# Second batch's operands replaced behind the token tiles; fourth chunk of the first mixture in another order

## The chip, the cores and the metric

The kernel runs on one core of a Trainium2 chip. The metric is device time in microseconds for one execution of the whole program. Engines are named as in the profile: PE is TensorE, PEld its weight loads, DVE is VectorE, ACT is ScalarE, POOL is GpSimd, SP is SyncE, which issues the DMAs.

## The reference, cut to what matters

An attention with a cluster mask, then two mixtures; every product is computed to float32 accuracy.

```python
def reference(...):
    x = _attn_ref(q, k, v, centroids)        # 2 batches x 8 heads, 768 tokens, head 64
    x = x.transpose(0, 2, 1, 3).reshape(1536, 512)
    h = x @ w_in                             # first mixture: 512 -> 2048
    r = np.maximum(h, 0.0)
    x = (r * r) @ w_out                      # 2048 -> 512
    p = domain_probs / (domain_probs.sum(-1, keepdims=True) + 1e-09)
    for e in range(4):                       # second mixture: 4 experts
        h = np.maximum(x @ w1[e], 0.0)       # 512 -> 1024
        out += p[:, e:e + 1] * (h @ w2[e])   # 1024 -> 512
```

## The kernel before

**Numbers as pairs.** An operand of TensorE is kept as a pair: hi is the value cast to TensorE's format (a cast on ScalarE), lo is what the cast left over (a subtraction on VectorE or GpSimd). A product is three matmuls: hi by hi, hi by lo, lo by hi. The h or l at the end of a tile's name says which half it is (wxh, wxl).

**Products of blocks.** The first matrix product of either mixture is done on a 2x2 split with seven block products instead of eight. For that, sums and differences of the blocks are needed on both sides. On the weights' side they are made by `w_sums` (four operations on GpSimd) and `w_mixed` (cast and subtraction into wyh and wyl); on the tokens' side by `t_sum`, with `r_hi` (cast, L943) and `r_lo` (subtraction, L946). The list `PROD` names the products: 1 takes RB11, 5 takes RT1, 6 RT2, 2 RB21, 7 RT3, 4 RT4, and 3 RB22.

**First mixture.** The 2048 hidden units are done in eight chunks (c = 0 to 7) of 256. `chunk(c)` is a generator of 15 pieces x = 0 to 14, each TensorE work (`prod1`, `gemm2`, `plain`) and what follows it. `gemm2` multiplies by w_out into banks 4 to 7, and VectorE adds those to x (L912). Between the pieces, hooks run that `put(c, x)` has hung there: the conversion of the next chunk's weights. `conv_in(c + 1)` prepares w_in (two blocks p and q, the sums, the two mixed operands mix), `conv_out(c + 1)` w_out (op and oq). The weights lie in memory as 64-bit words, so the conversion of a block (`split64`) is five integer operations on VectorE into a scratch tile (cva or fa), a cast on ScalarE, and a subtraction. `relu_c(c, tb, f)` takes one bank or sum: relu, square and cast on ScalarE (L845 to L847), the lo half on GpSimd (L848). `relu_c(c, 1, 1)` reads bank A of the chunk directly, and that bank is written again by `plain`, L856.

**Second mixture.** It goes through 32 groups n. Groups 0 to 15 are the 16 slices of 256 hidden units for the first 768 tokens (batch 0), 16 to 31 the same for batch 1 (NFQ is 16). A group's TensorE work stands in this order: product 4 of group n-1 (in `fourth`), product 1 of n, product 3 of n-1 (in `third`), then products 5, 6, 2 and 7 of n, each six matmuls of 128x384 (L878); then the six token tiles of group n-1, each six matmuls of 128x512 (L1040), whose result VectorE adds to x (L1050). Between them stand the preparation of the weights of group n+1: `raws` (wxh, wxl, L981), the sums (L200 to L203), `mixed` (wyh on ScalarE, wyl on GpSimd, L208 and L209); and wzl of group n, `second_lo` on GpSimd, L994. `c_copy` (L1009) is the copy out of bank A by ScalarE, `c_add` (L1012) an addition on VectorE.

**The second batch's operands.** Batch 1 needs the seven token operands anew. Four of them (RT3, RT1, RT2, RB21) go to a tile of their own, rt, during groups 11 to 14. The other three replace batch 0's in place, in xa: RB11, RT4 and RB22. Each may be overwritten only when the product that reads it has run for group 15. `swapped(n, i, eng)` does that in group 15 and at the start of group 16: RB11 behind product 1 of group 15, with the subtraction on VectorE; RT4 behind product 4 of group 15, the subtraction on GpSimd; RB22 behind product 3 of group 15, on VectorE. Products 4 and 3 of group 15 run within the head of group 16. RB11 is next read in group 16, by product 1; RT4 and RB22 are next read in the head of group 17, by products 4 and 3 of group 16.

**Order.** Nothing is reordered by a scheduler: each engine takes its instructions in the order in which the code is written, and waits on semaphores where data or a buffer is not there yet. What stands early in an engine's queue and waits holds up what stands behind it.

## Time and profile before

| | us |
|---|---|
| median of 3 runs | 1016.59 (1016.07 to 1016.91) |
| profiled execution, its own time | 1016.18 |
| its span in the profile | 1014.20 |
| TensorE busy | 1000.7 |
| VectorE busy | 733.2 |
| GpSimd busy | 620.0 |
| ScalarE busy | 561.3 |

The span is the stretch that the trace covers; the rest of the execution's time lies around it. Busy times are averages over very different parts: attention until about 260 us, the first mixture from then until about 509 us (L856 first at 264.4, the last L906 at 508.6), the second mixture behind that. Matmuls overlap, so a row's duration is not the distance to the next: within a group of this kernel, matmuls of 128x384 start some 0.17 us apart and those of 128x512 some 0.23 us. Where a row of a timeline ends in square brackets, the engine was idle ahead of it for that many microseconds, and the name behind the arrow is what it waited for.

### The profile page before, as it was taken

How to read it: one execution, taken by the hardware profiler on the slowest of the kernel's cores; microseconds unless marked ns; L12 is line 12 of the kernel's file. 1: busy time of each engine (PE TensorE's matmuls, PEld its weight loads, DVE VectorE, ACT ScalarE, POOL GpSimd, SP SyncE). 2: the span in 40 equal slices, each digit the busy share in tenths (PEclk: the TensorE clock that was granted, in tenths of full speed). 3: DMA queues.
4: the chain of work that ended last, by engine and by line, in shares of the span. 5: the costliest groups of instructions: out<-in, count | busy, mean ns of one | idle time of the engine just before them, and what ended most of it. 6: DMA issues, size and time to landing. Idle time of an engine off the chain costs nothing.

```text
span 1014.2 us, 15000 instructions
## 1 busy us (share of the span) xinstructions
PE 1000.7 (99%) x5467; PEld 892.1 (88%) x5467; DVE 733.2 (72%) x1114; ACT 561.3 (55%) x1131; POOL 620.0 (61%) x630
## 2 busy tenths in 40 slices
PE   8999999999999999999999999999999999999998
PEld 8999999999888878888889989899888998998997
DVE  7889899888899977988585554667665555555555
ACT  6888888988655644456454344344443444434431
POOL 5567677773326644346576766767667666676671
PEclk9999999999999999999999999999999999999999
DMA  7577876862112122212012122122223221211201
GB/s 184 126 155 178 191 179 157 187 140 71 42 42 83 46 80 83 77 49 82 22 42 84 43 83 83 42 84 63 63 83 104 84 79 47 83 63 62 84 22 63
DMA packets 74066, 89.65 MB, mean 88 GB/s; under 512 B 27316, under 2 KB 50248, under 8 KB 73992
## 3 DMA queue, kind: packets, MB, share of 16 engines
q1 hardware_dynamic: 73992, 88.69, 31.8%
q8 instruction: 43, 0.70, 0.3%
q14 instruction: 31, 0.25, 0.1%
HBM read 62.58 MB, written 3.19 MB: 65 GB/s over the span
## 4 chain that ended last, share of the span: by engine, by line
PE 71%; DVE 18%; POOL 4%; issue 2%; ACT 2%; DMA 1%; SPq 0%; POOLq 0%; DVEq 0%; ACTq 0%
PE bank L1040 26%; PE bank L878 24%; PE bank L906 5%; PE t L678 4%; PE s L645 4%; DVE ptl L684 2%; PE po L692 2%; PE po L694 2%; DVE nb L654 2%; DVE x L912 2%; PE bank L856 1%; DVE fa L177 1%; PE m L469 1%; DVE fa L172 1%; DVE cva L167 1%
## 5 line engine op out<-in xcount | busy, mean ns | idle before, releaser
L1050 DVE SCALAR_TENSOR_TENSOR x<-bank,pe_p,x 128x512 f32<-128x512 f32 x180 | 135.2, 751 | 69.6 <-PE bank L1040 69.3
L981 POOL TENSOR_TENSOR wxl<-raw,wxh 128x512 fp32r<-128x512 f32 x64 | 82.5, 1309 | 142.1 <-ACT wxh L980 142.1
L208 ACT CAST wyh<-raw 128x512 fp32r<-128x512 f32 x64 | 39.6, 621 | 152.9 <-POOL raw L201 120.0
L1040 PE MATMUL bank<-wzh,gb 128*128 128x512 f32 x384 | 121.2, 390 | 0.0
L1040 PE MATMUL bank<-wzh,ga 128*128 128x512 f32 x384 | 121.1, 390 | 0.0
L1012 DVE TENSOR_TENSOR fa<-bank,fa 128x384 f32<-128x384 f32 x96 | 53.3, 556 | 86.5 <-PE bank L878 57.3
L684 DVE TENSOR_TENSOR ptl<-t,pth 128x384 fp32r<-128x384 f32 x192 | 98.1, 549 | 17.9 <-ACT pth L683 17.4
L878 PE MATMUL bank<-xa,wxh 128*128 128x384 f32 (+1 forms) x392 | 103.9, 346 | 0.0
L654 DVE TENSOR_REDUCE nb<-s 128x1 f32<-128x768 f32 x96 | 90.9, 947 | 10.9 <-PE s L645 10.2
L878 PE MATMUL bank<-xa,wyh 128*128 128x384 f32 (+1 forms) x344 | 89.0, 339 | 1.6 <-ACT fa L1009 1.5
L665 ACT ACTIVATE p<-s,nb 128x768 f32<-128x768 f32 x96 | 87.9, 916 | 2.1 <-DVE nb L654 1.9
L683 ACT CAST pth<-t 128x384 fp32r<-128x384 f32 x192 | 83.9, 486 | 9.2 <-PE t L678 8.4
L678 PE MATMUL t<-identf,p 128*128 128x128 f32 x576 | 85.7, 276 | 1.2 <-DVE ptl L684 1.0
L645 PE MATMUL s<-k,q 80*128 80x384 f32 (+1 forms) x384 | 85.9, 345 | 0.5 <-DMA k<-ohm 0.5
L1040 PEld LDWEIGHTS bank<-wzh,gb 128*128 128x128 f32 x384 | 72.1, 188 | 14.7
L1040 PEld LDWEIGHTS bank<-wzh,ga 128*128 128x128 f32 x384 | 72.1, 188 | 14.7
L209 POOL TENSOR_TENSOR wyl<-raw,wyh 128x512 fp32r<-128x512 f32 x64 | 84.7, 1344 | 0.0
L1009 ACT COPY fa<-bank 128x384 f32<-128x384 f32 x96 | 46.0, 480 | 64.5 <-PE bank L878 64.4
L692 PE MATMUL po<-pth,vv 128*128 128x256 f32 x288 | 80.4, 309 | 0.0
L906 PE MATMUL bank<-gb,wzh 128*128 128x512 f32 x240 | 78.0, 391 | 0.3 <-DVE x L912 0.2
L678 PEld LDWEIGHTS t<-identf,p 128*128 128x128 f32 x576 | 67.1, 140 | 11.9 <-DVE ptl L684 9.0
L878 PEld LDWEIGHTS bank<-xa,wxh 128*128 128x128 f32 x392 | 72.2, 188 | 5.6
(279 smaller groups left out, 2648.8 us busy)
## 6 DMA issues: line engine op xcount, KB each, us to landing
raw<-in_moe_w_dram SPq DMA_DIRECT2D x64, 512.0 KB, 3.6
raw<-in_moe_w_in_dram SPq DMA_DIRECT2D x7, 1024.0 KB, 5.2
raw<-in_moe_w_out_dram SPq DMA_DIRECT2D x6, 1024.0 KB
k<-nkh SPq DMA_DIRECT2D x28, 192.0 KB, 3.4
q<-nqh SPq DMA_DIRECT2D x28, 192.0 KB, 4.1
nv<-in_v_dram SPq DMA_DIRECT2D x16, 192.0 KB, 3.8
out_dram<-x SPq DMA_DIRECT2D x12, 256.0 KB, 2.0
k<-nkl SPq DMA_DIRECT2D x14, 192.0 KB, 3.1
```

The source lines that it names most:

```text
L209: eng.tensor_tensor(lo, a[m], hi.bitcast(F32), op=ALU.subtract)
L645: nc.tensor.matmul(s[:, j, 0:HALF], stk[i, nq][:, t * 128:(t + 1) * 128], stk[i, nk][:, j * HALF:(j + 1) * HALF], start=first, stop=not first)
L654: nc.vector.tensor_reduce(out=nb, in_=s_ps[u][:, :, 0:HALF], axis=AX.XY, op=ALU.max, negate=True)
L665: nc.scalar.activation(p, s_ps.pop(u)[:, :, 0:HALF], AF.Exp, bias=nb_t.pop(u), accum_out=sums_t[hp][:, i % 2, t:t + 1])
L678: nc.tensor.transpose(tp[:, j], p_sb[u][:, half, j * 128:(j + 1) * 128], identf)
L683: return (lambda: nc.scalar.copy(dh, tp), lambda: nc.vector.tensor_tensor(dl, tp, dh.bitcast(F32), op=ALU.subtract))
L684: lambda: nc.vector.tensor_tensor(dl, tp, dh.bitcast(F32), op=ALU.subtract))
L692: nc.tensor.matmul(po_t[pr], vt[i][:, kt], pth[:, kt], start=(kt == 0), stop=False)
L878: nc.tensor.matmul(ps, w[:, ks], x(xx)[:, kt], start=(first and kt == 0 and z == 0), stop=(kt == 1 and z == 2), skip_group_check=True)
L906: nc.tensor.matmul(o, a[:, d], b, start=(ft == 0 and z == 0), stop=(ft == 1 and z == 2))
L1040: nc.tensor.matmul(o, a, w[:, f], start=(f == 0 and z == 0), stop=(f == 1 and z == 2))
L1050: nc.vector.scalar_tensor_tensor(out=acc, in0=o, scalar=pc, in1=acc, op0=ALU.mult, op1=ALU.add)
```

## The change

It has two parts. In the first mixture only chunk 3 is touched, with the preparation of chunk 4's weights in it. There the lo half of block q and the four sums go from GpSimd to VectorE; the relu of `relu_c(3, 1, 1)` is split: the relu itself stays behind product 4, and its square, cast and subtraction stand behind the mixed operands, at x = 9, where the cast and subtraction of the mixed operands now also stand; the first conversion of w_out moves from x = 9 to x = 10, and one cast of wzh from x = 12 to the start of chunk 4. In the second mixture the three calls of `swapped` stand behind the token tiles: RB11 at the end of group 15, RT4 and RB22 at the end of group 16, RT4 first. The engine of each stays what it was.

```diff
--- before.py
+++ after.py
@@ -192,11 +192,10 @@
 
     a_t = {}
 
-    def w_sums(a):
+    def w_sums(a, P=nc.gpsimd):
 
         a11, a12 = a[0][:, 0:2], a[0][:, 2:4]
         a21, a22 = a[1][:, 0:2], a[1][:, 2:4]
-        P = nc.gpsimd
         P.tensor_tensor(a22, a21, a22, op=ALU.add)
         P.tensor_tensor(a21, a11, a21, op=ALU.subtract)
         P.tensor_tensor(a11, a22, a11, op=ALU.subtract)
@@ -838,14 +837,20 @@
         x2_t = []
         relus = []
 
-        def relu2(src, c, tb, f):
+        def relu2_parts(src, c, tb, f):
             hh, hl = h_slot(c, tb, f)
             r = mp["r"][:, len(relus) % 2]
             relus.append(0)
             nc.scalar.activation(r, src, AF.Relu)
-            nc.scalar.activation(r, r, AF.Square)
-            nc.scalar.copy(hh, r)
-            nc.gpsimd.tensor_tensor(hl, r, hh.bitcast(F32), op=ALU.subtract)
+
+            def rest():
+                nc.scalar.activation(r, r, AF.Square)
+                nc.scalar.copy(hh, r)
+                nc.gpsimd.tensor_tensor(hl, r, hh.bitcast(F32), op=ALU.subtract)
+            return rest
+
+        def relu2(src, c, tb, f):
+            relu2_parts(src, c, tb, f)()
 
         def plain(c, m, ps, tb=0):
 
@@ -892,9 +897,12 @@
         def add1(c, k, b):
             nc.vector.tensor_tensor(mp["c1"][:, k], bank1(c, b), mp["c1"][:, k], op=ALU.add)
 
+        def relu_parts(c, tb, f):
+            src = bank1(c, "A") if (f, tb) == (1, 1) else mp["c1"][:, {(0, 1): 0, (0, 2): 1, (1, 2): 2}[f, tb]]
+            return relu2_parts(src, c, tb, f)
+
         def relu_c(c, tb, f):
-            src = bank1(c, "A") if (f, tb) == (1, 1) else mp["c1"][:, {(0, 1): 0, (0, 2): 1, (1, 2): 2}[f, tb]]
-            relu2(src, c, tb, f)
+            relu_parts(c, tb, f)()
 
         def gemm2(c, tb, ft, ns=range(4)):
             wh, wl = w_block(1, 2 * (c % 2) + ft)
@@ -1384,17 +1392,19 @@
 
             b = 2 * (c % 2)
             p, q = [split64(c // 2, 0, b + m, lambda shp, m=m: cv_p[m](shp),
-                            (nc.vector, nc.gpsimd)[m]) for m in range(2)]
+                            (nc.vector, nc.gpsimd)[m and c != 4]) for m in range(2)]
 
             def a():
                 return [a_t[c // 2, 0, b + m]["a"] for m in range(2)]
-            return p, q, [lambda: w_sums(a())], [
+            return p, q, [lambda: w_sums(a(), *([nc.vector] if c == 4 else []))], [
                 [lambda m=m: w_mixed(c % 2, m, a(), nc.gpsimd)] for m in range(2)]
 
         def conv_out(c, cvs=cv_p):
             return [
                 split64(c // 2, 1, 2 * (c % 2) + m, lambda shp, m=m: cvs[m](shp), nc.vector)
                 for m in range(2)]
+
+        split = []
 
         def chunk(c):
             yield lambda: prod1(c, 1), lambda: copy1(c, 0)
@@ -1406,7 +1416,8 @@
             yield lambda: c > 2 and gemm2(c - 1, 2, 0), None
             yield lambda: prod1(c, 7), lambda: (copy1(c, 2), add1(c, 2, "C"))
             yield lambda: gemm2(c - 1, 2, 1), lambda: c > 2 and relu_c(c, 2, 1)
-            yield lambda: prod1(c, 4), lambda: relu_c(c, 1, 1)
+            yield lambda: prod1(c, 4), lambda: (
+                split.append(relu_parts(c, 1, 1)) if c == 3 else relu_c(c, 1, 1))
             yield lambda: prod1(c, 3), lambda: (
                 add1(c, 1, "C"), relu_c(c, *((1, 0) if c == 2 else (2, 0))))
             yield lambda: plain(c + 1, 0, bank[3]), lambda: c > 2 and relu2(bank[3], c + 1, 0, 0)
@@ -1467,12 +1478,18 @@
                 put_load(c, 10, 4, 0)
                 put(3, [0], [[lambda: relu2(bank[3], 3, 0, 0)]])
             else:
-                put(c, (4, 5, 5, 5, 7, 7, 7, 7, 7, 7) if c == 3 else (1, 4, 4, 4, 5, 6, 6, 7, 7, 7), [
-                    p[0], p[2][0:1], q[0][0:3], p[2][1:2], q[0][3:5], q[1], sums2,
-                    [lambda c=c: relu_c(c, 1, 0)], *mix])
+                if c == 3:
+                    put(c, (4, 5, 5, 5, 7, 7, 7, 8, 8, 9, 9, 9), [
+                        p[0], p[2][0:1], q[0][0:3], p[2][1:2], q[0][3:5], q[2][0:1],
+                        [lambda: relu_c(3, 1, 0)], q[2][1:2], sums2, *mix, [lambda: split.pop()()]])
+                else:
+                    put(c, (1, 4, 4, 4, 5, 6, 6, 7, 7, 7), [
+                        p[0], p[2][0:1], q[0][0:3], p[2][1:2], q[0][3:5], q[1], sums2,
+                        [lambda c=c: relu_c(c, 1, 0)], *mix])
                 put_load(c, 7, c + 2, 0)
                 op, oq = conv_out(c + 1)
-                put(c, (9, 10, 11, 12), [op[0][0:3], op[0][3:5], oq[0][0:3], op[2][0:1]])
+                put(c, (10 if c == 3 else 9, 10, 11), [op[0][0:3], op[0][3:5], oq[0][0:3]])
+                put(*((c + 1, [0]) if c == 3 else (c, [12])), [op[2][0:1]])
             put(c + 1, (0, 0), [[lambda c=c: relu2(bank[c % 2], c + 1, 0, 1)],
                                 op[2][1:2] if c > 2 else []])
             put(*((c, [13]) if c > 3 else (c + 1, [0])), [oq[0][3:5]])
@@ -1549,16 +1566,14 @@
                     fq_load(3, 0)
                     fq_load(2, 1)
 
-        def swapped(n, i, eng):
-            if n == NFQ - 1:
-                r_hi(1, R_OF[i])
-                r_lo(1, R_OF[i], eng)
+        def swapped(i, eng):
+            r_hi(1, R_OF[i])
+            r_lo(1, R_OF[i], eng)
 
         def fourth(n):
             product(n, 4)
             h_hi(n, 1, 0)
             h_lo(n, 1, 0)
-            swapped(n, 4, nc.gpsimd)
             m = n - (NFQ - 6)
             if 0 <= m < 4:
                 r_hi(1, (RT3, RT1, RT2, RB21)[m])
@@ -1570,7 +1585,6 @@
         def last_relu(n):
             h_hi(n, 0, 1)
             h_lo(n, 0, 1)
-            swapped(n, 3, nc.vector)
 
         def group(n):
             prep = fq_prep(n + 1)
@@ -1579,7 +1593,6 @@
                 fourth(n - 1)
             product(n, 1)
             c_copy(n, 0)
-            swapped(n, 1, nc.vector)
             if n > 1:
                 third(n - 1)
             last_relu(n - 1)
@@ -1606,6 +1619,11 @@
             second_lo(n, nc.gpsimd)
             for t in range(2, NTT):
                 token_tile(n - 1, t)
+            if n == NFQ - 1:
+                swapped(1, nc.vector)
+            if n == NFQ:
+                swapped(4, nc.gpsimd)
+                swapped(3, nc.vector)
             fq_load(n + 3, 0)
             fq_load(n + 2, 1)
             if 0 <= m < 5 and m != 3:
```

In what follows the queues are shown, one engine at a time. The names are those of the code; [waits ...] are the semaphores, by the engine or DMA queue that raises them. Line numbers of the changed kernel are one lower at the sums and the mixed operands, five higher at the block products (L883) and eight higher behind those.

GpSimd, from the last subtraction of group 15's preparation to the head of group 16, before (xa is RT4's lo half):

```order
L209 TENSOR_TENSOR wyl<-raw,wyh 128x512 [waits PE_49,Activation_49]
L994 TENSOR_TENSOR wzl<-raw,wzh 128x1024 [waits DMAHW1_49]
L946 TENSOR_TENSOR xa<-x_4465,xa 128x768 [waits DVE_49,PE_49,Activation_49]
L981 TENSOR_TENSOR wxl<-raw,wxh 128x512 [waits DMAHW2_49,Activation_49]
L981 TENSOR_TENSOR wxl<-raw,wxh 128x256 [waits PE_49,Activation_49]
L200 TENSOR_TENSOR raw<-raw 128x2x128 [waits Pool_49]
```

The same one group later in the changed kernel, from the end of group 16 to the head of group 17:

```order
L208 TENSOR_TENSOR wyl<-raw,wyh 128x512 [waits Activation_49]
L208 TENSOR_TENSOR wyl<-raw,wyh 128x512 [waits PE_49,Activation_49]
L1002 TENSOR_TENSOR wzl<-raw,wzh 128x1024 [waits DMAHW3_49]
L954 TENSOR_TENSOR xa<-x_4465,xa 128x768 [waits DVE_49,Activation_49]
L989 TENSOR_TENSOR wxl<-raw,wxh 128x512 [waits DMAHW4_49,PE_49,Activation_49]
L989 TENSOR_TENSOR wxl<-raw,wxh 128x256 [waits PE_49,Activation_49]
```

RT4's lo half stood behind the wzl of group 15 and now stands behind that of group 16; it no longer waits for TensorE.

VectorE, from the end of group 14's work on the token tiles, before (xa is RB11's lo half, in the head of group 15):

```order
L1050 SCALAR_TENSOR_TENSOR x_4464<-bank_4462,pe_p,x_4464 128x2x256 [waits PE_49]
L1050 SCALAR_TENSOR_TENSOR x_4465<-bank_4463,pe_p,x_4465 128x2x256 [waits PE_49]
L940 TENSOR_TENSOR x_4465<-x_4465,x_4464 128x2x384
L1021 SCALAR_TENSOR_TENSOR gb<-bank_4456,gb 128x384 [waits Activation_49]
L946 TENSOR_TENSOR xa<-x_4464,xa 128x768 [waits PE_49,Activation_49]
L1012 TENSOR_TENSOR fa<-bank_4458,fa 128x384 [waits PE_49]
L1021 SCALAR_TENSOR_TENSOR gb<-fa,gb 128x384 [waits Activation_49]
```

VectorE in the changed kernel, at the end of group 15 and the start of group 16:

```order
L1058 SCALAR_TENSOR_TENSOR x_4464<-bank_4462,pe_p,x_4464 128x2x256 [waits PE_49]
L1058 SCALAR_TENSOR_TENSOR x_4465<-bank_4463,pe_p,x_4465 128x2x256 [waits PE_49]
L954 TENSOR_TENSOR xa<-x_4464,xa 128x768 [waits Activation_49]
L1029 SCALAR_TENSOR_TENSOR ga<-bank_4457,ga 128x384 [waits Activation_49]
L1020 TENSOR_TENSOR fa<-bank_4459,fa 128x384 [waits PE_49]
L1029 SCALAR_TENSOR_TENSOR ga<-fa,ga 128x384 [waits Activation_49]
```

The subtraction stood between the head's two operations in group 15 and now stands behind the last token tile's addition, ahead of the head of group 16.

VectorE in chunk 3, from the last addition of a run of four on, before (cva and fa are the scratch tiles; L161 begins the conversion of w_out):

```order
L912 TENSOR_TENSOR x_4465<-bank_4463,x_4465 128x512 [waits PE_49]
L161 TENSOR_SCALAR cva<-raw 128x512 [waits DMAHW2_49,Pool_49]
L164 TENSOR_SCALAR cva<-cva 128x512 [waits DVE_49]
L167 TENSOR_SCALAR cva<-cva 128x512 [waits DVE_49]
L893 TENSOR_TENSOR fa<-bank_4458,fa 128x512 [waits PE_49]
L172 SCALAR_TENSOR_TENSOR cva<-raw,cva 128x512 [waits DVE_49]
L177 SCALAR_TENSOR_TENSOR cva<-raw,cva 128x512 [waits DVE_49]
```

The same place in the changed kernel:

```order
L920 TENSOR_TENSOR x_4465<-bank_4463,x_4465 128x512 [waits PE_49]
L186 TENSOR_TENSOR wxl<-fa,wxh 128x512 [waits Activation_49]
L199 TENSOR_TENSOR fa<-fa 128x256 [waits DVE_49]
L200 TENSOR_TENSOR fa<-cva,fa 128x256 [waits DVE_49]
L201 TENSOR_TENSOR cva<-fa,cva 128x256 [waits DVE_49]
L202 TENSOR_TENSOR cva<-cva 128x256 [waits DVE_49]
L898 TENSOR_TENSOR fa<-bank_4458,fa 128x512 [waits PE_49]
L161 TENSOR_SCALAR cva<-raw 128x512 [waits DMAHW2_49,Pool_49]
L164 TENSOR_SCALAR cva<-cva 128x512 [waits DVE_49]
L167 TENSOR_SCALAR cva<-cva 128x512 [waits DVE_49]
```

Five operations came in ahead of the conversion, and the addition of bank C (L893, now L898) moved ahead of it too.

## Rows read from the trace of the kernel before

**Rows 1.** Page, part 1: busy us, share of the span, number of instructions.
```profile
PE 1000.7 (99%) x5467; PEld 892.1 (88%) x5467; DVE 733.2 (72%) x1114; ACT 561.3 (55%) x1131; POOL 620.0 (61%) x630
```

**Rows 2.** Waits of TensorE, whole span: us in total, times, longest.
```profile
PE bank L856 <- ACT fa L845: 1.8, 1, 1.8
PE bank L878 <- ACT fa L1009: 1.5, 1, 1.5
...
PE bank L878 <- ACT fa L890: 0.4, 1, 0.4
```

**Rows 3.** Timeline, chunk 3: start, us, line, operation, tiles [idle before <-releaser].
```profile
364.08 2.48 DVE L912 TENSOR_TENSOR x<-bank,x 128x512 f32<-128x512 f32 x4
...
366.05 0.62 ACT L847 CAST gb<-fa 128x512 fp32r<-128x512 f32 x1
...
370.69 1.28 POOL L209 TENSOR_TENSOR wyl<-cva,wyh 128x512 fp32r<-128x512 f32 x1
...
372.00 1.47 DVE L161 TENSOR_SCALAR cva<-raw 128x512 int32<-128x512 int32 x1 [5.44 <-POOL wyl L209]
```

**Rows 4.** Timeline, chunks 3 and 4: adds and idle time of VectorE, matmuls behind.
```profile
389.18 2.48 DVE L912 TENSOR_TENSOR x<-bank,x 128x512 f32<-128x512 f32 x4
...
390.15 0.39 PE L906 MATMUL bank<-gb,wzh 128*128 128x512 f32 x1
...
396.61 0.69 DVE L893 TENSOR_TENSOR fa<-bank,fa 128x512 f32<-128x512 f32 x1 [1.17 <-ACT fa L890]
...
415.06 0.50 PE L906 MATMUL bank<-gb,wzh 128*128 128x512 f32 x1 [0.23 <-DVE x L912]
```

**Rows 5.** Timeline of VectorE: one subtraction of two SBUF tiles, at two places.
```profile
345.49 1.78 DVE L186 TENSOR_TENSOR wzl<-raw,wzh 128x512 fp32r<-128x512 f32 x1
...
361.55 0.69 DVE L186 TENSOR_TENSOR wxl<-cva,wxh 128x512 fp32r<-128x512 f32 x1
```

**Rows 6.** Timeline of TensorE: first matmuls of groups 15, 16 and 17.
```profile
734.39 0.51 PE L878 MATMUL bank<-xa,wxh 128*128 128x384 f32 x2
...
751.63 0.51 PE L878 MATMUL bank<-xa,wxh 128*128 128x384 f32 x2
...
767.13 0.51 PE L878 MATMUL bank<-xa,wxh 128*128 128x384 f32 x2
```

**Rows 7.** Timeline, group 15: VectorE's subtraction and GpSimd's beside it.
```profile
737.62 2.40 POOL L994 TENSOR_TENSOR wzl<-raw,wzh 128x1024 fp32r<-128x1024 f32 x1
...
738.00 2.83 DVE L946 TENSOR_TENSOR xa<-x,xa 128x768 fp32r<-128x768 f32 x1 [1.02 <-ACT xa L943]
```

**Rows 8.** Timeline around the start of group 17: ScalarE's cast, GpSimd's subtractions.
```profile
767.14 2.54 POOL L209 TENSOR_TENSOR wyl<-raw,wyh 128x512 fp32r<-128x512 f32 x2
...
767.21 0.62 ACT L208 CAST wyh<-raw 128x512 fp32r<-128x512 f32 x1 [1.01 <-POOL raw L203]
...
769.64 2.40 POOL L994 TENSOR_TENSOR wzl<-raw,wzh 128x1024 fp32r<-128x1024 f32 x1
```

**Rows 9.** Lines 946 and 943: duration in ns, min/median/max, first and last start.
```profile
L946 DVE TENSOR_TENSOR xa<-x,xa x6: 944/1228/2834, 504.5 to 756.9; 128x768 fp32r<-128x768 f32 x6
L946 POOL TENSOR_TENSOR xa<-x,xa x3: 1837/1846/2201, 496.9 to 756.5; 128x768 fp32r<-128x768 f32 x3
...
L943 ACT CAST xa<-x x9: 817/833/841, 492.2 to 756.0; 128x768 fp32r<-128x768 f32 x9
```

**Rows 10.** Start and end: matmuls; window row: us, busy, granted clock, DMA, GB/s.
```profile
2.65 2.72 PE L1071 MATMUL po<-identr 128*128 128x256 f32 x11 [2.65 <-DVE sel L295]
5.16 1.47 PE L347 MATMUL s<-identf,nk 128*128 128x128 f32 x6
6.44 0.85 PE L347 MATMUL t<-identf,nq 128*128 128x128 f32 x6
...
1009.81 0.39 PE L1040 MATMUL bank<-wzh,ga 128*128 128x512 f32 x1
...
1013.00:1014.20 1.20, 0.00 (x0) 0.67 0.00 0
```

## The prediction

> **What bounds the kernel now.** I read the page's busy shares first: TensorE is busy for 99% of the span, so any time it gains or loses goes to the end almost one to one [rows 1]. Then I read the list of who TensorE waited for. Of its few waits, three stand where the change works: 1.8 us on a relu of the fourth chunk (chunk 3), 0.4 us on a copy at the start of chunk 4, and 1.5 us on a copy in group 15 of the second mixture, the last group of the first batch [rows 2]. If all three went and nothing came in their place, the gain would be 3.7 us and about 0.3 us of restarting the pipeline. The timelines of the other engines say what comes in their place, and that is where I spent the time.
>
> **Part 1: the chunk.** The relu that reads bank 1 now runs ahead of two conversions, so the bank is free before TensorE asks for it, and the copy now runs ahead of the conversion of wzh. Both waits of 1.8 and 0.4 us should go. But VectorE is the next limit. From 372.00 on, when the lo half of wyl has freed the tile cva [rows 3], VectorE works without a gap until 395.4 (its next idle time ends at 396.61 and is 1.17 us long, rows 4), and in that stretch it adds the product's banks to x. Of the run of four adds at 389.18 the first ends near 389.86, and TensorE writes that bank again at 390.15: 0.3 us to spare. One chunk later, at 415.06, TensorE already waits for such an add [rows 4]. So TensorE, freed of 2.2 us in chunk 3, runs into these adds, and what part 1 is worth is how much earlier VectorE's stretch starts or how much shorter it gets, not the 2.2 us.
>
> When does it start? Five operations are new on VectorE ahead of it: the lo half of wxl (0.69 us alone) and four sums of half its width, which no row shows; I bound each by 0.35 us (half) and 0.69 us. They follow the four adds that start at 364.08 and end at 366.6. GpSimd begins its first difference when the cast of 366.05 ends, 366.7 [rows 3], and a second 1.9 us later, as ScalarE needs three passes of 0.63 us for each. VectorE's subtraction of two SBUF tiles takes 0.69 us alone, and 1.78 us where it began during a GpSimd operation [rows 5]: it waited until that one was over. So of the four sums two wait behind GpSimd's two differences (1.3 us each), and the sums end at about 366.6 + 0.6 + 1.2 + 0.3 + 1.4 + 0.3 + 0.9 = 371.1 (lo half, wait, sum, wait, sum, two sums). Then come a cast (0.6) and the lo half of wyl (1.3): the stretch starts at 373.1, 1.1 us later than before. In return the add of bank C (0.6 us, a quarter of a run of adds) is done ahead of it, and GpSimd's last difference meets the adds from PSUM and one short subtraction instead of a longer collision (about 0.8 us less). Sum: 1.1 - 0.6 - 0.8 = **-0.3 us**. Bounds: with no collision in the sums -1.3 us, with one more collision in the stretch +1.0 us. I take -0.3, since rows 5 show the collision for the same kind of operation.
>
> The Trainium skill (SBUF — State Buffer, Who interferes with whom) says that VectorE with two SBUF inputs and GpSimd take turns on one port, whole instructions at a time. By that rule the value is the -0.3 us used here; without it -1.3 us, and the end 1.0 us earlier.
>
> **Part 2: the operands of the second batch.** Three casts on ScalarE and three subtractions (two on VectorE, one on GpSimd) move from just behind the product that last reads the old operand to the end of the group. Nothing is added; each has the same price as before. What counts is how soon TensorE needs them.
>
> *Removed.* In group 15 VectorE's subtraction of xa took 2.83 us because GpSimd's wyl and wzl held it up until 740.02 [rows 7]; alone it takes 0.94 us [rows 9]. Behind it the copy that TensorE waited for was late. Group 15 lasts from 734.39 to 751.63, 17.24 us, and group 16 to 767.13, 15.50 us [rows 6]. Without the subtraction in its head, group 15 should last 15.5 us: **-1.7 us**.
>
> *RB11, first operand of group 16.* Its cast now stands behind the last cast of wyh, and TensorE's second product of group 16 reads it, 1.04 us (six matmuls, some 0.17 us apart in rows 6) after the group starts. Against a group boundary, wyh's last cast starts at +0.08 (767.21 against 767.13) and takes 0.62 us; the cast of xa (0.83 us) ends at +1.4. VectorE's subtraction starts there, but GpSimd's two wyl operations fill +0.0 to +2.5 [rows 8], so it waits for the second and ends 0.81 us behind it (740.83 against 740.02, rows 7): +3.3. The second matmul of that product needs it and would have run at +1.2. **+2.2 us**; without the collision +1.2.
>
> *RT4, first operand of group 17.* Its subtraction stays on GpSimd, and there it now stands behind wyl, wyl and wzl of the end of group 16. These run after the boundary: the two wyl take +0.0 to +2.5, wzl 2.40 us from +2.5 [rows 8]. RB22's subtraction on VectorE, ready at +2.2 after two casts, gets its turn at +2.5 and delays wzl to about +3.2, so wzl ends at +5.6. Then xa's own 1.84 us [rows 9]: ready at +7.4. The very first product of group 17 reads it with its second matmul, wanted at +0.2. **+7.3 us** (6.6 if RB22 doesn't hold up wzl). Queued behind on GpSimd is only wxl, which is not due before late in the group: GpSimd is idle for some 4 us there. RB22 itself is ready at +3.4 and costs nothing next to this. Nothing later can give the time back, since TensorE waits hardly anywhere else.
>
> *The clock.* That is over 7 us in which TensorE does one matmul. At the program's end the granted clock is 1.00 until after 1013 and 0.67 on average over the last 1.2 us, which puts its fall to half (from 2.4 to 1.2 GHz) at 1013.4, 3.2 us after the last matmul. At the start TensorE works from 2.65 on; six matmuls of a kind take 1.47 us at 5.16, and six of the same size 0.85 us at 6.44 [rows 10]. So it worked 3.8 us (2.65 to 6.44) before it ran at full speed, and lost about half of these. I expect the clock to fall in the stall and to come back as it did at the start: 3.8 us at about half speed, **+1.8 us**; bounds 0 (it holds) and 2.6.
>
> **Sum.** -0.3 - 1.7 + 2.2 + 7.3 + 1.8 = +9.3 us. The profiled execution took 1016.18 us (span 1014.20), which gives 1025.5; the median of the three runs is 0.4 above it, and a median is what I predict: 1016.59 + 9.3 = **1025.9 us**.
>
> **Rivals.** *The clock holds through the stall.* Everything else as above: 1024.1 us. For it: the stall is broken by one matmul near +1.5, and only one fall is in the trace; against it: it is twice as long as the idle time before that fall. The Trainium skill (TensorE: Matmul & The Clock Gate, Part 1) has the clock at 1.2 GHz after idling until there has been sustained work, and the trace agrees at both ends; by that rule it is 1025.9. *GpSimd is less far behind.* If only xa and wzl stand after the boundary, the wyl pair being done before it, the big stall is some 4.8 us, too short to be sure of the clock: about 1022. Against it: the pair starts at the boundary in rows 8, as the sums ahead of it are tied to the same group's products. *The other side: faster.* The stall in group 15 goes (-1.7), part 1 gives 1.3 to 2.5, and the moved subtractions are in time: 1012.4 to 1013.6 us. This needs GpSimd to reach xa before TensorE reaches group 17; it decides at the boundary, where wzl would have to be over, and rows 8 show it ending 4.9 us later (772.04 against 767.13). That the order in the queues is not what the change says is shut out by its rows.
>
> **How the numbers follow.** Forecast 0.71, clock holds 0.15, GpSimd less late 0.08, faster 0.03, no change within 0.2% (about what a measurement of this kernel can tell from none) 0.03. The range takes in the clock's rival with part 1 at its best (1024.1 - 1.0 = 1023.1) and the forecast with part 1 at its worst and the clock's upper bound, not both in full (1025.9 + 1.8 = 1027.7): 1022.9 to 1027.8. Faster by over 0.2% 0.03, within 0.2% 0.03, slower 0.94.
>
> **What would show it.** In the profile after, TensorE's list of waits should be led by L883, the product, on GpSimd's xa of L954 (lines of the changed kernel), 5 to 7 us in one piece, at the start of group 17, and a wait of some 2 us on VectorE's xa in the second product of group 16; the waits on the relu and on the copy of group 15 should be gone. In chunks 3 and 4 new waits on the adds (L920), 1 to 2 us in all, should eat what the relu's wait gives back. Matmuls behind the long wait should start nearly twice as far apart as the 0.17 us of rows 6 for a few us, and the granted clock of that stretch should be below 1. If the xa on GpSimd ends before TensorE gets to group 17, the forecast is wrong as a whole.

## The result

The changed kernel took 1025.77 us in the median of 4 runs (1024.73 to 1026.23), the kernel before 1016.41 (1016.07 to 1016.91, 4 runs beside them). The ratio is 1.009, with a 95% interval of 1.0073 to 1.0108: 9.4 us slower. The forecast was 1025.9.

### The profile page after: what moved, and what is told of

Read it like the earlier page. It is cut to its first block, busy times and chain, and to the rows that moved or that the text cites. A ratio compares the mean times of both kernels' runs of the same rounds, so it can differ in the third digit from the quotient of the medians.

```text
span 1024.0 us, 15000 instructions
## 1 busy us (share of the span) xinstructions
PE 1004.5 (98%) x5467; PEld 894.7 (87%) x5467; DVE 734.2 (72%) x1119; ACT 561.2 (55%) x1131; POOL 617.3 (60%) x625
## 4 chain that ended last, share of the span: by engine, by line
PE 71%; DVE 19%; POOL 4%; issue 3%; ACT 2%; SPq 0%; DMA 0%; POOLq 0%; DVEq 0%; ACTq 0%
PE bank L1048 25%; PE bank L883 24%; PE bank L914 5%; PE t L677 4%; PE s L644 4%; DVE ptl L683 2%; PE po L691 2%; PE po L693 2%; DVE nb L653 2%; DVE x L920 2%; PE bank L861 1%; PE m L468 1%; DVE cva L167 1%; DVE fa L177 1%; POOL wyl L208 1%
## 5 line engine op out<-in xcount | busy, mean ns | idle before, releaser
L883 PE MATMUL bank<-xa,wxh 128*128 128x384 f32 (+1 forms) x392 | 105.9, 350 | 8.4 <-POOL xa L954 5.4
L883 PE MATMUL bank<-xa,wyh 128*128 128x384 f32 (+1 forms) x344 | 89.2, 339 | 0.1
L883 PEld LDWEIGHTS bank<-xa,wxh 128*128 128x128 f32 x392 | 73.1, 190 | 15.2 <-POOL xa L954 5.7
## 6 DMA issues: line engine op xcount, KB each, us to landing
raw<-in_moe_w_in_dram SPq DMA_DIRECT2D x7, 1024.0 KB, 5.1
raw<-in_moe_w_out_dram SPq DMA_DIRECT2D x6, 1024.0 KB
```

The lines of the kernel that those rows point to most:

```text
L883: nc.tensor.matmul(ps, w[:, ks], x(xx)[:, kt], start=(first and kt == 0 and z == 0), stop=(kt == 1 and z == 2), skip_group_check=True)
```

## The profile after

TensorE is busy for 1004.5 us (before: 1000.7, [rows 1]) in a span of 1024.0. Its list of waits (us in total, times, longest) of the changed kernel, to be held against [rows 2]:

```profile
PE bank L883 <- POOL xa L954: 5.4, 1, 5.4
...
PE bank L914 <- DVE x L920: 1.9, 3, 1.0
PE bank L883 <- ACT xa L951: 1.6, 2, 1.3
PE bank L883 <- DVE xa L954: 1.5, 1, 1.5
```

The three waits of [rows 2] are gone. In their place stand the moved operands (GpSimd's xa, its cast on ScalarE, VectorE's xa) and VectorE's additions. In what follows, what a stall costs is the distance between the starts of the two matmuls around it less the usual one (0.17 us for 128x384, 0.23 for 128x512); it is some 0.2 us more than the wait in the list.

The timeline of the changed kernel from the end of group 16 into group 17 shows the largest of them (start, us, engine, line, operation, tiles, idle time before):

```profile
767.40 0.39 PE L1048 MATMUL bank<-wzh,ga 128*128 128x512 f32 x1
769.10 0.45 PE L883 MATMUL bank<-xa,wxh 128*128 128x384 f32 x1 [1.31 <-ACT xa L951]
774.95 0.69 PE L883 MATMUL bank<-xa,wxh 128*128 128x384 f32 x1 [5.41 <-POOL xa L954]
...
776.71 0.84 PE L883 MATMUL bank<-xa,wxh 128*128 128x384 f32 x2
...
780.60 0.51 PE L883 MATMUL bank<-rt,wyh 128*128 128x384 f32 x2
...
767.62 2.50 POOL L208 TENSOR_TENSOR wyl<-raw,wyh 128x512 fp32r<-128x512 f32 x2
770.07 3.06 POOL L1002 TENSOR_TENSOR wzl<-raw,wzh 128x1024 fp32r<-128x1024 f32 x1
773.10 1.79 POOL L954 TENSOR_TENSOR xa<-x,xa 128x768 fp32r<-128x768 f32 x1
...
769.81 1.13 DVE L954 TENSOR_TENSOR xa<-x,xa 128x768 fp32r<-128x768 f32 x1 [1.24 <-ACT xa L951]
```

Group 17 could have started at 767.63. One matmul runs at 769.10, when ScalarE's cast is there; the second runs at 774.95, right after GpSimd's xa, which stood behind two wyl and wzl and ended at 774.89, 7.26 us behind the group's start. wzl took 3.06 us instead of the 2.40 of [rows 8], since VectorE's subtraction of RB22 got its turn between wyl and wzl. Behind the stall two matmuls take 0.84 us, later 0.51.

The granted clock of TensorE tells why (window: us, TensorE busy, matmuls, granted clock, DMA share, GB/s):

```profile
771.00:773.00 2.00, 0.00 (x0) 0.91 0.77 261
773.00:774.80 1.80, 0.00 (x0) 0.50 0.35 28
...
776.00:778.00 2.00, 2.00 (x8) 0.50 0.19 67
...
779.00:780.00 1.00, 1.00 (x6) 0.77 0.00 0
780.00:785.00 5.00, 5.00 (x30) 1.00 0.00 0
```

0.91 over two microseconds at the levels 1.0 and 0.5 (2.4 and 1.2 GHz) means that the clock fell at 772.6, 3.5 us after the start of the one matmul in the stall; 0.77 over the last means that it rose at about 779.5, 4.5 us after the work began again. Twelve matmuls in that stretch start 0.32 us apart instead of 0.17, and the first 0.48: 2.1 us in all.

The head of group 16, with RB11:

```profile
749.85 0.51 PE L883 MATMUL bank<-xa,wxh 128*128 128x384 f32 x2
...
753.25 0.44 PE L883 MATMUL bank<-xa,wxh 128*128 128x384 f32 x1 [1.48 <-DVE xa L954]
...
749.86 2.52 POOL L208 TENSOR_TENSOR wyl<-raw,wyh 128x512 fp32r<-128x512 f32 x2
...
751.31 1.88 DVE L954 TENSOR_TENSOR xa<-x,xa 128x768 fp32r<-128x768 f32 x1 [0.51 <-ACT xa L951]
```

VectorE's subtraction is ready to start at 751.31 but ends at 753.19, 0.81 us behind GpSimd's second wyl (752.38); alone it takes 0.94 [rows 9]. The Trainium skill (SBUF — State Buffer, Who interferes with whom) says that a VectorE instruction with two SBUF inputs and a GpSimd instruction that reads SBUF exclude each other; these 1.88 us agree with it, as the sums in chunk 3 do:

```profile
367.68 1.40 DVE L199 TENSOR_TENSOR fa<-fa 128x256 f32<-128x256 f32 x1
369.12 0.43 DVE L200 TENSOR_TENSOR fa<-cva,fa 128x256 f32<-128x256 f32 x1
...
373.48 1.50 DVE L161 TENSOR_SCALAR cva<-raw 128x512 int32<-128x512 int32 x1 [1.45 <-POOL wyl L208]
...
382.20 0.50 PE L914 MATMUL bank<-gb,wzh 128*128 128x512 f32 x1 [0.96 <-DVE x L920]
...
389.96 0.50 PE L914 MATMUL bank<-gb,wzh 128*128 128x512 f32 x1 [0.67 <-DVE x L920]
```

A sum of half width takes 0.43 us alone and 1.40 beside a GpSimd subtraction. VectorE's conversion begins at 373.48 (before: 372.00, [rows 3]), and in chunk 4 TensorE waits for the additions at 382.20 and 389.96; the second of these matmuls had 0.3 us to spare before [rows 4].

## The experiments

All differences are against the kernel before, run beside, unless another kernel is named. One execution each, except where a number of runs is told.

### The chunk's part alone

```diff
 # the changed kernel, with the three calls back at their old places
+            if n == NFQ - 1:
+                swapped(4, nc.gpsimd)     # in fourth
 ...
+            if n == NFQ - 1:
+                swapped(3, nc.vector)     # in last_relu
 ...
+            if n == NFQ - 1:
+                swapped(1, nc.vector)     # behind product 1
 ...
-            if n == NFQ - 1:
-                swapped(1, nc.vector)
-            if n == NFQ:
-                swapped(4, nc.gpsimd)
-                swapped(3, nc.vector)
```

> Only the chunk's part of the change; the second batch's operands stay where they were. My theory: the waits on the relu (1.97 us lost in the trace of before) and on the copy (0.52 us) go, and waits on VectorE's adds of nearly the same sum come in chunk 3 and at the start of chunk 4, so that TensorE reaches chunk 6 0.3 to 0.5 us earlier than before, counted from the start of chunk 3; the time is within 0.5 us of before. Rival: alone, without the other part, it brings what the two waits cost, 2.2 to 2.5 us. The wait of 1.6 us in group 15 stays in both.

Measured: 1015.93 against 1016.55. In its trace the stalls that stood at the relu and the copy (1.97 and 0.52 us) are gone; in their place TensorE loses 1.14 and 0.85 us to VectorE's additions, both in chunk 4 (the theory had one of them in chunk 3). From 297 to 510 us it gained 0.35 us on the kernel before, read in its trace, since the time of one execution alone settles no difference so small. For the rest my theory holds: the part is worth about 0.4 us, not what the removed waits had cost.

### The sums back on GpSimd

```diff
-   (nc.vector, nc.gpsimd)[m and c != 4]
+   (nc.vector, nc.gpsimd)[m]
-   [lambda: w_sums(a(), *([nc.vector] if c == 4 else []))]
+   [lambda: w_sums(a())]
```

> The chunk's part alone, with the four sums and the lo half of block q left on GpSimd as before; the order of the relu and the copies is that of the change. My theory: GpSimd then has some 4.3 us more ahead of the first wyl, so the scratch tile is free 1.5 to 2 us later than in the changed kernel; VectorE, although it has five operations less, adds later, and TensorE's waits on the additions grow by 1 to 2 us over those of the changed kernel. Rival: VectorE's own work was the limit, and without the five operations the waits on the adds shrink.

Measured: 1019.18, that is 3.3 us over the chunk's part alone (one execution each). The direction is the theory's; the size is above it. The timeline:

```profile
375.24 1.29 POOL L208 TENSOR_TENSOR wyl<-cva,wyh 128x512 fp32r<-128x512 f32 x1 [0.73 <-ACT wyh L207]
...
376.57 1.51 DVE L161 TENSOR_SCALAR cva<-raw 128x512 int32<-128x512 int32 x1 [9.35 <-POOL wyl L208]
...
381.07 0.58 ACT L895 COPY fa<-bank 128x512 f32<-128x512 f32 x1
```

VectorE idles 9.35 us and starts 3 us later than in the changed kernel, not 1.5 to 2. TensorE's waits on the additions grow by 0.9 us (2.8 against 1.9 in its list), a little less than the theory's 1 to 2. And a wait came that I had not listed: the late conversion of the mixed operands holds up ScalarE, whose copy at 381.07 costs TensorE another 2.4 us. So with the new order of the relu alone the chunk would have been slower; the sums on VectorE are what makes that order bearable.

### One operand moved at a time

```diff
 # from the kernel before; in each, one of the three calls moves, the others stay
+            swapped(n, 1, nc.vector)         # behind the token tiles: RB11
+            swapped(n - 1, 4, nc.gpsimd)     # or RT4
+            swapped(n - 1, 3, nc.vector)     # or RB22
```

RB11 alone:

> From the kernel before, only RB11 is moved to the end of group 15; RT4, RB22 and the chunk stay. My theory: the wait of 1.6 us in group 15 goes, and in group 16 the second product waits 0.3 to 0.5 us for ScalarE's cast and 1.5 to 1.8 us for VectorE's subtraction, which takes 1.9 us because GpSimd's pair of wyl is under way: +0.5 us in all, no fall of the granted clock. Rival: the subtraction was long only because RT4 and RB22 stand behind it, and alone it takes 0.95 us: -0.4 us.

Measured: 1017.32 against 1016.55, +0.8. In the trace the stall of group 15 is gone; in group 16 TensorE loses 0.43 us to the cast and 1.73 to VectorE's subtraction, the same as in the changed kernel. Groups 15 and 16 together take 0.5 us longer than before in the traces, which is the theory's figure. The lateness is RB11's own.

RT4 alone:

> From the kernel before, only RT4 is moved to the end of group 16. My theory (GpSimd's queue): the subtraction of 1.84 us starts when wyl, wyl and wzl are over, 4.9 us behind the group's start without RB22's subtraction in wzl's way, and ends at +6.7 us; TensorE loses 6.6 us, then the granted clock falls to half and some 12 matmuls of 128x384 cost 0.15 us more each, 1.8 us: +8.4 us in all. Rival: the length of the stall comes from VectorE's and ScalarE's work of RB22 beside it; without that, under 4 us and no fall of the clock.

Measured: 1024.79 against 1016.55, +8.2. GpSimd's queue in its timeline:

```profile
767.08 2.50 POOL L209 TENSOR_TENSOR wyl<-raw,wyh 128x512 fp32r<-128x512 f32 x2
769.54 2.34 POOL L994 TENSOR_TENSOR wzl<-raw,wzh 128x1024 fp32r<-128x1024 f32 x1
771.83 1.80 POOL L946 TENSOR_TENSOR xa<-x,xa 128x768 fp32r<-128x768 f32 x1
```

Without RB22's subtraction beside it, wzl takes 2.34 us instead of 3.06, xa ends 0.7 us earlier, and the stall is 4.96 instead of 5.68 us. Nearly the whole loss of the change is this one instruction.

RB22 alone:

> From the kernel before, only RB22 is moved to the end of group 16. In the changed kernel its lateness is hidden behind RT4's. My theory: its cast ends at +1.4 us behind the group's start, its subtraction waits for the second wyl until +2.5 and ends at +3.3; product 3 of group 16 wants it at +2.3: +1.0 us, clock at full. Rival: the subtraction gets in between the two wyl and nothing waits: 0.0 us.

Measured: 1016.91 against 1016.55. In the trace product 3 loses 1.13 us to VectorE's subtraction, as expected; single executions differ by nearly a microsecond, so the time alone would not settle it. In the changed kernel this is hidden behind RT4. This run showed something else as well. The clock fell where nothing was changed, behind the wait on the relu in chunk 3:

```profile
372.63 0.73 PE L856 MATMUL bank<-xa,wxh 128*128 128x512 f32 x2 [1.82 <-ACT fa L845]
...
374.00:374.50 0.50, 0.50 (x4) 0.68 0.00 0
374.50:375.00 0.50, 0.50 (x3) 0.50 0.00 0
...
377.50:378.00 0.50, 0.50 (x3) 0.91 0.00 0
378.00:378.50 0.50, 0.50 (x4) 1.00 0.00 0
```

It fell at about 374.2, 1.5 us after TensorE had gone back to work, and rose at 377.6. Yet it cost nothing here: the waits on the copy at 381 and on the addition at 415 [rows 2, 4] and a smaller one on an addition at 446 are missing in this run, and from 296 to 516 us TensorE took 219.3 us, as in the kernel before (219.2). Where VectorE's additions set the pace, slow matmuls only eat the waits for them.

### The second price of the stall: the clock

```diff
+            if n == NFQ + 1:
+                for _ in range(7):      # 42 matmuls into a free bank, result unused
+                    block_product(0, 5, bank[4][:, 0:HALF], lambda x: r_op(R_OF[5], x, 1), True)
             if n > 1:
                 fourth(n - 1)
```

> The changed kernel with 42 more matmuls of 128x384 (seven times a block product into a bank that is free then, its result unused) put ahead of product 4 of group 16, so that TensorE works through the stall: 42 times 0.173 us are 7.3 us, as long as the stall. My theory: the slow matmuls behind the stall owe to the clock, which falls because TensorE idles. With the filling the granted clock stays at 1.00, all matmuls behind keep 0.173 us, and the kernel is 1.8 to 2.1 us faster than the changed one although it does more. Rival: the matmuls behind the stall are slow for another reason (operands just written, other engines' traffic); then the time is that of the changed kernel or up to 0.3 us longer.

Measured: 1024.09 (4 runs) against 1016.57, that is 7.5 us slower than before and 1.7 faster than the changed kernel, with 7.3 us of work more. In the window of the former stall:

```profile
772.00:776.00 4.00, 4.00 (x24) 1.00 0.61 201
776.00:780.00 4.00, 4.00 (x25) 1.00 0.05 20
```

Product 4 begins at 774.76, just as GpSimd's xa gets ready (774.88), and its matmuls and those behind it keep their 0.17 us. So the slow matmuls were not due to the operands just written: they were the clock's doing, and TensorE's idling what made it fall.

### The first price: GpSimd's queue

```diff
             second_lo(n, nc.gpsimd)
+            if n == NFQ:
+                second_lo(n, nc.gpsimd)     # wzl a second time
```

> The changed kernel with GpSimd's subtraction wzl of group 16 done twice, 2.40 us more in the queue ahead of RT4's subtraction. My theory (GpSimd's queue sets the end of the stall): the stall grows by 2.4 us, the loss by the clock stays as it is, since the clock has fallen anyway: 2.4 us slower than the changed kernel. Rival (another engine or the data set the end): no change.

Measured: 1029.11, 3.3 us slower than the changed kernel. The wait on GpSimd's xa in TensorE's list:

```profile
PE bank L883 <- POOL xa L954: 7.8, 1, 7.8
```

It is 2.4 us longer, the length of one wzl: the queue sets the end. The rest is the clock, which I had taken as unchanged: it rose at about 783.3, 5.7 us after TensorE went back to work instead of 4.5, and 16 matmuls were slow instead of 12, 0.6 us; some 0.3 us lie within the scatter of single runs.

```diff
+            if n == NFQ:
+                swapped(4, nc.gpsimd)       # RT4 ahead of wzl
             second_lo(n, nc.gpsimd)
 ...
-                swapped(4, nc.gpsimd)       # and no longer behind the token tiles
```

> The changed kernel with RT4's subtraction still on GpSimd but ahead of wzl. My theory: it starts behind the second wyl at +2.5 us, or at +3.2 if RB22's subtraction takes the turn, and ends at +4.4 to +5.0; the second matmul of product 4 idles for 2.9 to 3.5 us. In the changed kernel the granted clock fell some 3 us after the last matmul, so the fall is on the edge: 2.4 to 3.0 us faster than the changed kernel if the clock falls, 4.2 to 5.0 if not. Rival: RT4's subtraction is held up by something else than wzl; then nothing changes.

Measured: 1023.99, 1.8 us faster than the changed kernel, less than the 2.4 to 3.0 expected with a fall of the clock. GpSimd's timeline:

```profile
768.50 2.50 POOL L208 TENSOR_TENSOR wyl<-raw,wyh 128x512 fp32r<-128x512 f32 x2
770.95 2.52 POOL L954 TENSOR_TENSOR xa<-x,xa 128x768 fp32r<-128x768 f32 x1
773.43 2.38 POOL L1002 TENSOR_TENSOR wzl<-raw,wzh 128x1024 fp32r<-128x1024 f32 x1
```

xa comes right behind the wyl, ends at 773.47, 5.0 us behind the group's start, and the stall is 3.38 instead of 5.68 us. That is the 2.3 us which the queue explains. The gain was smaller since the clock fell twice in this run: here, and in group 16 at 753.5 (1.6 us lost), behind the short stall on RB11, where it had not fallen in the profile of the changed kernel.

```diff
-                swapped(4, nc.gpsimd)
+                swapped(4, nc.vector)       # RT4's subtraction on VectorE
```

> The changed kernel with RT4's subtraction on VectorE, ahead of RB22's. My theory: it starts when the second wyl is over and ends at +3.3 us behind the group's start, so the first long wait is 1.3 us for the cast and 1.8 us for the subtraction; RB22's follows either at once or behind wzl, which costs product 3 nothing or 1.1 us. No idle stretch of TensorE is longer than 2 us and the granted clock stays at 1.00: 5.4 to 6.5 us faster than the changed kernel, 2.9 to 4.0 us slower than before. Rival: VectorE's subtraction has to let all three of GpSimd's operations pass, and is ready at +5.8: 3 us faster than the changed kernel at most.

Measured: 1022.40, 3.4 us faster than the changed kernel. The stalls were as expected: 1.47 us on the cast, 1.72 on RT4's subtraction, 0.86 on RB22's. What I had excluded was a fall of the clock behind waits this short. So I ran the same kernel again:

> The same kernel as in the run with RT4's subtraction on VectorE, in more executions. In that run the granted clock fell to half for some 3.4 us in group 16, although TensorE had waited there only twice, under 2 us each; that cost about 1.6 us, and the run was 3.4 us faster than the changed kernel instead of 5.4 to 6.5. Theory A: whether the clock falls behind a stall of that length differs from execution to execution; then the times form two groups some 1.6 us apart, the faster near 1020.8 with a mean clock of 1.000 over the execution and the slower near 1022.4 with 0.998. Theory B: it falls every time in this kernel; then all times lie within 0.8 us of 1022.4, with 0.998. Theory C: that run was an exception; then all lie near 1020.8.

Measured: 1021.87 (5 runs, 1021.13 to 1022.65, mean clocks 0.996 to 0.998), 5.6 us slower than before, 3.9 faster than the changed kernel. The granted clock, first in the earlier trace, then in the new one:

```profile
753.00:753.50 0.50, 0.50 (x4) 1.00 0.56 168
753.50:754.00 0.50, 0.50 (x3) 0.53 0.98 324
...
756.50:757.00 0.50, 0.50 (x3) 0.55 0.78 254
757.00:757.50 0.50, 0.50 (x5) 1.00 1.01 393
```

```profile
753.00:757.00 4.00, 4.00 (x24) 1.00 0.55 153
...
770.50:771.50 1.00, 0.93 (x5) 0.90 0.33 110
771.50:773.00 1.50, 1.50 (x6) 0.50 0.79 277
...
774.50:776.00 1.50, 1.50 (x10) 0.93 0.73 269
```

One program, two executions: in the first the clock fell in group 16 and not in group 17, in the second in group 17 and not in group 16, both times while TensorE was working again. All five runs show a mean clock of 0.996 to 0.998, which speaks for a fall in each (the profiled executions that fall only at the program's end show 0.999 to 1.000), but they are spread over 1.5 us and do not form two groups. So of my three theories A is right in that it differs from execution to execution where the clock falls, and wrong in its two groups of times. B has the fall in every run, but two of the times lie 1.0 and 1.3 us from its 1022.4; C is out. The Trainium skill (TensorE: Matmul & The Clock Gate, Part 1) describes the lower level as that of an idle engine and the higher as that of a busy one; these falls came 0.7 to 1.6 us after the engine was busy again, so these two levels alone don't tell on which stalls to reckon with a fall. What the rows show: it came behind stalls of 1.7 to 2 us in some executions and not in others, not behind the one of 2.4 us with the sums back on GpSimd, and behind the four of 3.4, 5.0, 5.7 and 8.1 us each time. What decides between executions of the same instructions stays open here. The kernel before is not free of it: 4 of its 17 executions that ran beside the versions below have a mean clock of 0.997 or 0.998, at 1016.03 to 1017.03 us, so a fall in them cost nothing that the time shows; where it came no trace says.

### What can be kept

```diff
 # the chunk's part of the change; RT4 and RB22 at their old places; RB11 within group 15:
             prep[0]()
+            if n == NFQ - 1:
+                r_hi(1, RB11)
             token_tile(n - 1, 0)
 ...
             h_lo(n, 1, 1)
+            if n == NFQ - 1:
+                r_lo(1, RB11, nc.vector)
             prep[2]()
```

> The chunk's part of the change, RT4 and RB22 as in the kernel before, and RB11 within group 15: its cast behind those of wxh, its subtraction on VectorE behind the second token tile's addition, where VectorE idles 0.6 us between two additions. My theory: the wait of 1.6 us in group 15 goes and none comes in its place, since the subtraction ends some 2 us ahead of group 16; with the chunk's part 2.0 us faster than before. Rival: VectorE's additions behind it come late and token tiles wait, or the cast delays ScalarE's work: gain under 1 us.

Measured: 1014.09 (11 runs) against 1016.37 (17 runs), ratio 0.9977 (0.9969 to 0.9986). VectorE's timeline in group 15, and the start of group 16:

```profile
746.03 1.49 DVE L954 TENSOR_TENSOR xa<-x,xa 128x768 fp32r<-128x768 f32 x1
747.44 2.08 DVE L1058 SCALAR_TENSOR_TENSOR x<-bank,pe_p,x 128x512 f32<-128x512 f32 x3
...
749.93 0.51 PE L883 MATMUL bank<-xa,wxh 128*128 128x384 f32 x2
```

The subtraction meets one of GpSimd's sums (1.49 us instead of 0.94) and pushes an addition back, which nobody waits for; it is ready at 747.5, 2.4 us ahead of group 16. The idea of the change, to take RB11 out of the head of group 15, was sound; only the other end was too late.

```diff
-   [lambda m=m: w_mixed(c % 2, m, a(), nc.gpsimd)] for m in range(2)]
+   # c == 4: the cast of the first mixed operand as before, its subtraction on VectorE at x = 10
```

> As the kernel with RB11 within group 15, and in chunk 3 the lo half of the first mixed operand (1.3 us on GpSimd) on VectorE, behind the addition of bank C. My theory: the loss that is left in chunks 3 and 4 (1.1 and 0.8 us) is VectorE's conversion of w_out, which starts when the scratch tile is free; here that is at once after a subtraction of 0.7 us, and GpSimd stands in the way of one conversion step less, so the adds come 0.5 to 1.7 us earlier and the kernel is that much faster than the one it is made from. Rival: VectorE's stretch is as long as before because of the added operation; no gain, or 0.7 us slower.

Measured: 1013.11 (7 runs) against 1016.37, ratio 0.9969 (0.9958 to 0.9981), some 1.0 us faster than the one above. VectorE's timeline in chunk 3:

```profile
371.22 0.69 DVE L210 TENSOR_TENSOR wyl<-cva,wyh 128x512 fp32r<-128x512 f32 x1
371.94 1.41 DVE L161 TENSOR_SCALAR cva<-raw 128x512 int32<-128x512 int32 x1
```

The idle time of 1.45 us ahead of the conversion is gone, and TensorE's first stall on the additions in chunk 4 falls from 1.16 to 0.42 us; the second stays (0.85). This version is 3.3 us faster than the kernel before and 12.7 us faster than the changed one.

## Why the prediction was right, and where it was lucky

**The whole.** Counted in the trace, the parts give -0.5 in the chunk, -1.7 in group 15, +2.3 in group 16 and +9.3 in group 17 (the stall and the clock): +9.3 us, as forecast. (The spans of the two traces differ by 9.8 us; another 0.5 us of that lies ahead of 297 us, where nothing was changed.) No term was off by more than 0.4 us, but that the errors cancel to less than 0.1 is luck.

**The chunk** (forecast -0.3, trace -0.35 to -0.5): right by its own steps. The waits went, VectorE's stretch started about a microsecond later, and the additions ate the gain. Both waits on them came in chunk 4, none in chunk 3. A sum alone was sized at 0.3 us and one held up at 1.5 and 1.7; they took 0.43 and 1.40. The terms written down for the end of the sums add up to 371.3, not 371.1; no other step changes by that.

**Group 15** (-1.7): from its first matmul (at 734.35 in the timeline of after) to that of group 16 (749.85) it took 15.50 us against 17.24 in [rows 6]. Of the two operations named as the cause before only wzl held the subtraction up: the wyl pair was over at 737.7 and the subtraction ready at 738.00.

**RB11** (+2.2): 0.42 on the cast, 1.74 on the subtraction and 0.1 of restart. The collision with the second wyl came as read from [rows 7, 8].

**RT4** (+7.3, measured 7.15, of which 1.47 stand ahead of the first matmul): ready 7.26 us behind the group's start, forecast +7.4; wzl taking 3.06 us instead of 2.40 through RB22's turn was part of the sum, and the run with RT4 alone shows that piece by itself.

**The clock** (+1.8, measured 2.1): the reading holds at both ends, the size with some luck. I took the slow matmuls at the start of the program [rows 10] for a clock at half. The window row of that stretch in the trace of before shows a granted clock of 1.00 (fourth column behind the window), which seems to speak against it:

```profile
2.65:5.00 2.35, 2.35 (x11) 1.00 0.85 252
```

But the trace's record of the clock has its first entry only at 6.48 us; ahead of it there is none, and the 1.00 stands for a missing entry. The matmuls show the change. With RB22 alone the first entry is at 5.54, and the six matmuls of s, 1.47 us in [rows 10], take

```profile
5.16 1.01 PE L347 MATMUL s<-identf,nk 128*128 128x128 f32 x6
```

In the changed kernel it is at 8.04, and the six of t, 0.85 us in [rows 10], take

```profile
6.44 1.49 PE L346 MATMUL t<-identf,nq 128*128 128x128 f32 x6
```

In all 14 traces the first entry lies between 5.5 and 8.5 us, and matmuls of 128x128 start 0.21 us apart ahead of it and 0.11 behind it, nearly the ratio of 0.32 to 0.17 behind the stall. So TensorE did begin at half clock. The luck is in the size: the first matmul starts at 2.65 in each, so the rise came 2.9 to 5.8 us behind it, and the trace at hand happened to show 3.8; behind the stall it came after 4.5. The upper bound of 2.6 us was given without a sum. The fall at the program's end was as good a guide: 3.2 us after the end of the last matmul there, 3.1 us after that of the last one here.

**A chance that I did not see.** The sum counted no fall of the clock behind RB11's stall of 1.7 us, and named no such risk. The profile of the changed kernel agrees, but two other kernels with the same stall show a fall behind it. A forecast with that risk in it would have reached about 1.6 us further up for some executions; the range ended 1.9 above the forecast, so it would have held them.

**The rivals.** That the clock holds is refuted by its own record and by the filled kernel. That GpSimd is less far behind is refuted by the wyl pair at 767.62, right at the boundary. Faster would have needed wzl over at the boundary; it ended at 773.1.

## What to carry to other kernels

Before moving an operation out of the way of one stage, look up what its engine has in its queue at the new place and when the next reader wants it: here the wait removed cost 1.7 us, and the same operand's next reader paid 2.3, another's 7.2 and then the clock. An engine that hardly waits is often next to a second one that hardly waits: removing its stalls is worth only what the second one has to spare, so shorten that one's stretch too. For RB11 the right place was the middle of the group, where both its engine and its reader have time; the other two operands were not tried there.

## What the runs showed of the hardware

A fall of TensorE's clock can come behind stalls of under 2 us, and while TensorE is working again: at 374.2, 753.5 (twice) and 771.3 in four executions, for some 3.4 us each; in other executions of the same instructions it didn't come. In group 16 it cost 1.6 us, and nothing in a chunk where TensorE would have waited for VectorE anyway. At the start of the program TensorE runs at half clock (matmuls of 128x128 start 0.21 us apart instead of 0.11) until 5.5 to 8.5 us, differently from execution to execution; the window rows show 1.00 there because the trace has no entry of the clock so early. VectorE's subtraction of 0.94 us takes 1.88 when it begins during a GpSimd subtraction, and GpSimd's next one, which then has to wait, 3.11 instead of 2.40 (group 16 of the changed kernel; 3.06 in group 17): both engines pay.
